# A fused attention and mixer kernel: the second channel product's seven products in transposed form, wider sums, packed constants

## The chip, the cores and the metric

The kernel runs on one core of a Trainium2 chip. The metric is device time in microseconds (us) of one execution, the median of several runs; lower is better. The core's engines are TensorE (PE: matmuls, with its weight loads shown apart as PEld), VectorE (DVE), ScalarE (ACT), GpSimd (POOL) and SyncE (SP, which here only issues transfers). Matmuls write PSUM, a small memory that VectorE and ScalarE read; all else lies in SBUF, 128 partitions wide. Transfers are carried by 16 DMA engines.

## What is computed

The inputs are u and v (8 batches, 3008 positions, 256 channels), z (8, 3008, 64) and four weights. An attention without softmax is gated by u, and a mixer follows that mixes first over positions (tokens), then over channels:

```python
# _attn_ref
scale = 1.0 / S
scores = scale * np.matmul(z, z.transpose(0, 2, 1))
attn = np.maximum(scores, 0.0) ** 2
out = np.matmul(attn, v)
return (u * out).astype(np.float32)
...
# _moe_ref, x is the result above
xt = x.transpose(0, 2, 1)
h = np.maximum(xt @ w_tok1, 0.0) @ w_tok2          # (3008 -> 256 -> 3008)
u = x + h.transpose(0, 2, 1)
h2 = np.maximum(u @ w_ch1, 0.0) @ w_ch2            # (256 -> 1536 -> 256)
return (u + h2).astype(np.float32)
```

Operands are bf16, sums in PSUM are float32.

## The kernel before

**Tiling.** The 3008 positions of a batch are six blocks of 512 (the last has 448); `b` counts batches, `q` query blocks, `g` key blocks. A key tile is 128 positions, four of them make a group.

**Attention.** `score_run` (line 448) makes score tiles in PSUM (line 465), `relu` (480) takes them to an `at` tile with ScalarE, `square` (509) squares them on VectorE (line 511). Scores are symmetric, so a block of one (q, g) is also used for (g, q): `flip` (558) turns a whole `at` tile into an `fl` tile by a transposing transfer on SyncE's queue (line 562), and blocks on the diagonal are completed by smaller turns (`flip_tiles`, line 554). `av_matmul` (684) accumulates attention times v (line 692). `finish` and `gate` (804, 836) add the two halves and multiply by u into `xT`, channels in partitions. `turn_x` (879) turns that back into an `x_pair`, positions in partitions.

**Token mixing.** The product with w_tok1 is done by a scheme with seven products of half-size blocks in place of eight. The scheme needs sums of blocks: `token_sums` (949) makes them of the weights once, `x_sums` (908) of the data, four subtractions for each block into a `d_pair` (line 921). `tok1` (1008) runs the products into one PSUM pair `a_ps` (line 1031); `collect_a` (1040) adds the parts into a float32 tile `a_f` and writes the relu into a tile of its own, `a_sb`. `tok2` (1099) multiplies by w_tok2 into `h_ps` (line 1105), its `add` (line 1114) adds to `xT`. `turn_u2` turns the sum into `u_sb`, positions in partitions.

**Channel mixing.** `ch1` (1149) makes 256 hidden channels at a time, in six steps `c2` (line 1162), and ScalarE writes their relu into `h2pre` tiles (line 1201), each of which holds two steps (a channel group `d`). The product with w_ch2 is again the seven-product scheme, for every block but the very last of the kernel: `mix_weights` (974) makes the weight sums once (line 990, eight subtractions), `make_sums` (1227) the sums of the hidden values, four instructions for each group into an `hsum` tile (lines 1241, 1246, 1250, 1253). `product` (1272) runs one of the products k = 1 to 7, each 12 matmuls of 128 columns (six in the last block), into one of two PSUM banks, `xb` or `zb` (line 1298), and `collect` (1309) adds the bank to the output tile `ro` with VectorE (line 1334) after each. When all seven are in, the tile is stored (line 1339). The rest goes through plain products (`ch2`, line 1398, stores at line 1436).

A hidden tile is cut in four for the scheme: by channels into two halves `r` and by positions into two halves `m`. Before, `m` runs over alternate tiles of 128 positions:

```python
            return st["h2", q, d].rearrange("p (j r) w -> p j r w", r=2)[
                :, :, r, :2 * n * P].rearrange("p j (i m s) -> p j i m s", m=2, s=P)[:, :, :, m, :]
```

**What sets the order.** There is no dynamic scheduler on the chip. While the program is built, a planner keeps estimated clocks for each engine: `push` (364) puts an operation for ScalarE, VectorE or SyncE on a list with an estimated ready time, a busy time and a latency; `run_engines` issues those whose time has come; the loop from line 1778 picks TensorE's next work by what the estimates say is ready. The products of a block and the hidden steps of the next are one list in a fixed order, line 1510, where 0 stands for a hidden step of the next block and 1 to 7 for a product:

```python
                for k in ORDER_LAST[b % 2] if q == NQ - 1 else (0, 0, 1, 2, 0, 6, 5, 0, 7, 3, 0, 4):
```

**Buffers and queues.** SBUF tiles come from pools with a set number of places, counted in `ROOM`: 11 `fl`, 9 `xT`, 6 `at`, 6 `h2`. The `fl` places hold flipped attention tiles, `x_pair`, `d_pair`, `hsum`, `ro` and `a_f` in turn; `release` gives a place back at an estimated time. SyncE's queue carries all turns and the stores, in the planner's order. GpSimd's queue carries the loads of u, v, z and the weights; `after` (122) puts a copy of one column into a tile `mark` in front of a load, so that the load starts only when that column is there. The z tiles of a batch are loaded into `zs` (26 columns of 64 values each, the first and the last zero) and turned by `turn_z` (136) in pairs of transfers that start at tile k and k + 1 (line 141).

**Constants.** `mark` is 128 bytes per partition and comes first, then the weights, their sums, an identity matrix `ident` and `zs`.

Of the kernel before, what the change touches and what calls it, by code (L numbers as in the profile page):

```python
# [57 lines left out]
def kernel(  # L58
# [29 lines left out]
    sb = ctx.enter_context(tc.tile_pool(name="sb", bufs=2))  # L88
    psum = ctx.enter_context(tc.tile_pool(name="psum", bufs=2, space=bass.MemoryType.PSUM))
# [7 lines left out]
    mark = consts.tile([P, 32], F32)  # L97
# [83 lines left out]
    def turn_on_pe(zr, zp):  # L181

        for t in range(GK):
            nc.tensor.matmul(  # L184
                zp[:, t, :], zr[:, t].rearrange("p h d -> p (h d)"), ident[:],
                start=(t == 0), stop=True, skip_group_check=True)
# [15 lines left out]
    def fill(n, bank):  # L202

        for _ in range(n):
            nc.tensor.matmul(
                bank, zero[:, :P], zero[:], start=True, stop=True, skip_group_check=True)
# [672 lines left out]
    def turn_x(b, q, t):  # L879
# [10 lines left out]
        push("dve", t + slack, 0.21, 0.36, lambda t: x_sums(b, q, t), first=-1,  # L890
# [17 lines left out]
    def x_sums(b, q, t):  # L908


        if q % 2 == 0:
            d_pairs[b, q] = new_pair(xd_home(b, q), [3, QW // P // 2, P], "d_pair")
# [4 lines left out]
        steps = [(d[:, 1], high[:, 1], low[:, 1]), (low[:, 1], low[:, 1], low[:, 0]),  # L917
                 (d[:, 0], high[:, 1], low[:, 1]), (d[:, 2], high[:, 0], d[:, 0])]
# [55 lines left out]
    def mix_weights(t):  # L974
# [5 lines left out]
        for c in range(2):  # L980
# [3 lines left out]
                (to[:, 0], low[:, :, 1, :], low[:, :, 0, :]),  # L984
                (to[:, 2], high[:, :, 1, :], low[:, :, 1, :]),
                (to[:, 1], high[:, :, 1, :], to[:, 0]),
                (to[:, 3], high[:, :, 0, :], to[:, 1])]

        def step(t):
            nc.vector.tensor_sub(*steps.pop(0))  # L990
# [5 lines left out]

    BORROW = 3
    VERY_LAST = (B - 1, NQ - 1, CHT // 2 - 1)
    ORDER_LAST = ((1, 2, 6, 5, 7, 0, 3, 4), (1, 2, 6, 5, 0, 7, 3, 0, 4))

    def add_mixer(b):
# [6 lines left out]
        def tok1(q, end):  # L1008
# [10 lines left out]
            for i in range(n):  # L1019
# [4 lines left out]
                    ((1, 1), w[:, j, 0, 1, :], xp[:, 1, i, 0, :]),  # L1024
                    ((0, 2), w_sum_sb[:, 1, j, :], d[:, 0, i, :]),
                    ((1, 2), w_sum_sb[:, 0, j, :], d[:, 1, i, :]),
                    ((0, 3), w_sum_sb[:, 2, j, :], xp[:, 1, i, 1, :]),
                    ((1, 0), w[:, j, 1, 1, :], d[:, 2, i, :]),
# [8 lines left out]
            if q == NQ - 1:  # L1037
                home = "fl" if b else "h2"

                def collect_a(t):  # L1040
# [35 lines left out]
                    def relu_a(m, t):  # L1076
# [7 lines left out]
                        if len(made) == 2:  # L1084
                            recent[0] = to[:, :1]
                            if b:
                                release("fl", [1], max(made))
                            else:
                                live["h2"] -= 1

# [8 lines left out]
        def tok2(q, end):  # L1099
# [9 lines left out]
            def add(t):  # L1109
# [13 lines left out]
                u_done[q].t = t  # L1123
                st["turned", q] = push("sp", t, 1.25, 5.5, lambda t: turn_u2(q, t), first=1,
                                       room=lambda: has_room(("us",)) and (
                                           q <= HALF or goal[0] > (b, 1 + HALF)))
            ring.append((push("dve", end + 0.21, 1.12, 1.25, add, first=2), slot))

# [20 lines left out]
        def ch1(q, c2, borrowed, end):  # L1149
# [64 lines left out]
            if c2 == CHT // 2 - 1:  # L1214
                release("xT", xT_uses[q])

# [4 lines left out]
        def tiles_of(q, d, r, m):  # L1221

            n = pairs_of(q)
            return st["h2", q, d].rearrange("p (j r) w -> p j r w", r=2)[
                :, :, r, :2 * n * P].rearrange("p j (i m s) -> p j i m s", m=2, s=P)[:, :, :, m, :]

        def make_sums(q, d, t):
# [6 lines left out]
            def kind(k):  # L1234
                return sums["s"][:, k, :, :n, :]

            def add1(t):
                home, n_home = take_home(q)
                sums["s"] = sb.tile([P, 4, 2, 2, P], BF16, tag=home, name="hsum", bufs=n_home)
                st["sum", q, d] = sums["s"]  # L1240
                nc.vector.tensor_add(kind(0), tiles_of(q, d, 0, 1), tiles_of(q, d, 1, 1))  # L1241
                push("dve", t - 0.05, busy, busy + 0.15, add3, done=s_done[q, d, 2])
# [679 lines left out]
```

## Time and profile before

| | us |
|---|---|
| median of 3 runs | 1113.02 |
| lowest, highest | 1112.36, 1117.03 |
| span of the profiled execution, first to last instruction | 1110.5 |
| TensorE busy in it | 1105.7 |
| VectorE busy | 782.5 |
| ScalarE busy | 669.4 |
| GpSimd busy | 164.3 |

The profile is one execution; for that one it gives the span and no time outside it, so the median is set beside the span. Every view below comes from this execution. A row of a group names the line, the engine, the operation, output and inputs, the shape (partitions x elements, type) and the count; then the busy time in us and the mean of one in ns; then the idle time just before them and what ended it. A row of waits gives who waited for whom, us in total, times and the longest. A row of a timeline gives start and duration in us. The chain of waits is followed back from the last instruction, so its shares say which engine set the time.

### The profile page before, as it was taken

The numbers are of one execution on the slowest core, as the hardware profiler recorded it, in microseconds if no ns is written. First come the engines' busy times: TensorE is split into PE (matmuls) and PEld (weight loads), VectorE is DVE, ScalarE is ACT, GpSimd is POOL, SyncE is SP. The second block draws the span as 40 slices with busy tenths as digits, with TensorE's granted clock in tenths as the row PEclk, the third lists the DMA queues.
The fourth block names the chain that finished last, engine by engine and source line by source line (L and its number), as shares of the span: only waits on it lengthen the run. The fifth ranks groups of instructions, "written<-read, shape, count | busy, mean of one in ns | idle before, by whom it ended". The sixth has DMA issues, their size and how long they took to land.

```text
span 1110.5 us, 27244 instructions
## 1 busy us (share of the span) xinstructions
PE 1105.7 (100%) x11073; PEld 683.8 (62%) x11073; DVE 782.5 (70%) x1888; ACT 669.4 (60%) x843; POOL 164.3 (15%) x382
## 2 busy tenths in 40 slices
PE   9999999999999999999999999999999999999998
PEld 3444575766557665576556865557655676556676
DVE  6889865975758857588566885578756777556775
ACT  7999555645854567545665456653666536743454
POOL 5320110221003110032100311003210120000100
PEclk9999999999999999999999999999999999999999
DMA  9999947796977969779697797967979678693222
GB/s 177 155 194 164 192 98 143 141 174 134 191 133 141 180 148 174 133 147 203 135 183 119 131 214 139 172 123 152 202 154 170 111 148 182 127 164 93 67 58 96
DMA packets 465725, 165.54 MB, mean 149 GB/s; under 512 B 433024, under 2 KB 448960, under 8 KB 465600
## 3 DMA queue, kind: packets, MB, share of 16 engines
q1 hardware_dynamic: 436208, 131.11, 58.6%
q0 software_dynamic: 28880, 32.32, 21.2%
q8 instruction: 86, 1.41, 0.5%
q10 hardware_dynamic: 512, 0.38, 0.1%
q14 instruction: 39, 0.32, 0.1%
HBM read 65.40 MB, written 24.64 MB: 81 GB/s over the span
## 4 chain that ended last, share of the span: by engine, by line
PE 99%; DMA 1%; issue 0%; POOL 0%; DVE 0%; POOLq 0%
PE acc L692 42%; PE hp L1162 22%; PE xb L1298 11%; PE zb L1298 8%; PE sc L465 6%; PE h_ps L1105 4%; PE a_ps L1031 3%; PE op L1398 2%; PE first_acc L609 1%; DMA v_sb<-in_v_dram 1%; PE zp L184 0%; PE up L1700 0%; DVE res L1433 0%; POOL ident masks.py:199 0%; POOL ident masks.py:197 0%
## 5 line engine op out<-in xcount | busy, mean ns | idle before, releaser
L1201 ACT ACTIVATE h2pre<-hp 128x1024 bf16<-128x1024 f32 (+1 forms) x287 | 278.5, 1008 | 204.0 <-PE hp L1162 171.5
L692 PEld LDWEIGHTS <-v_sb 64*128 64x128 bf16 x4418 | 246.3, 94 | 210.9
L692 PE MATMUL acc<-at,v_sb 64*128 64x512 bf16 (+1 forms) x2738 | 340.9, 375 | 0.0
L503 ACT ACTIVATE at<-sc 128x1024 bf16<-128x1024 f32 (+1 forms) x290 | 286.6, 1027 | 62.5 <-PE sc L465 54.8
L1162 PE MATMUL hp<-xT,w_ch_sb 128*128 128x512 bf16 (+1 forms) x1152 | 274.7, 375 | 0.0
L511 DVE TENSOR_TENSOR at<-at 128x1024 bf16<-128x1024 bf16 (+1 forms) x290 | 198.2, 687 | 103.8 <-ACT at L503 99.9
L692 PE MATMUL acc<-fl,v_sb 64*128 64x512 bf16 (+1 forms) x1680 | 192.5, 367 | 0.0
L1162 PEld LDWEIGHTS <-w_ch_sb 128*128 128x128 bf16 x1152 | 105.6, 98 | 98.1 <-issue 3.0
L1298 PEld LDWEIGHTS <-hsum 128*128 128x128 bf16 x2088 | 124.4, 98 | 18.2 <-issue 0.3
L465 PE MATMUL sc<-zT 64*128 64x512 bf16 (+1 forms) x732 | 131.8, 359 | 0.2 <-ACT zT L1750 0.2
L1298 PEld LDWEIGHTS <-h2pre 128*128 128x128 bf16 x1566 | 95.5, 98 | 20.1
L820 ACT COPY cp<-acc 128x512 f32<-128x512 f32 (+1 forms) x94 | 54.9, 584 | 77.8 <-PE acc L692 66.8
L826 DVE TENSOR_TENSOR cp<-acc,cp 128x512 f32<-128x512 f32 (+1 forms) x94 | 63.5, 676 | 50.7 <-ACT cp L820 50.1
L1241 DVE TENSOR_TENSOR hsum<-h2pre 128x512 bf16<-128x512 bf16 (+1 forms) x141 | 56.1, 402 | 40.7 <-ACT h2pre L1201 39.4
L491 ACT ACTIVATE at<-sc 128x512 bf16<-128x512 f32 (+3 forms) x152 | 56.2, 447 | 41.5 <-PE sc L465 41.0
L1298 PE MATMUL xb<-w_mix_sb,hsum 128*128 128x128 bf16 x1044 | 73.7, 219 | 0.0
L1334 DVE TENSOR_TENSOR ro<-xb,u_sb 128x256 f32<-128x256 f32 (+1 forms) x141 | 56.5, 401 | 22.5 <-PE xb L1298 20.5
L542 DVE TENSOR_TENSOR at<-at 128x512 bf16<-128x512 bf16 (+3 forms) x152 | 41.5, 321 | 38.2 <-ACT at L491 38.2
L465 PEld LDWEIGHTS <-zT 64*128 64x128 bf16 x732 | 42.8, 94 | 41.2 <-issue 3.6
L124 POOL CAST mark<-at 128x1 f32<-128x1 bf16 x24 | 8.2, 342 | 372.5 <-DVE at L511 372.5
L846 DVE TENSOR_TENSOR xT<-cp,uT 128x512 bf16<-128x512 f32 (+1 forms) x94 | 62.5, 665 | 0.9
L1253 DVE TENSOR_TENSOR hsum<-h2pre,hsum 128x512 bf16<-128x512 bf16 (+1 forms) x141 | 56.6, 401 | 2.3
(89 smaller groups left out, 968.4 us busy)
## 6 DMA issues: line engine op xcount, KB each, us to landing
out_dram<-ro SPq DMA_DIRECT2D x40, 512.0 KB, 3.0
v_sb<-in_v_dram POOLq DMA_DIRECT2D x40, 256.0 KB, 4.6
ur<-in_u_dram POOLq DMA_DIRECT2D x40, 256.0 KB, 4.9
w_tok_sb<-in_moe_w_tok_dram POOLq DMA_DIRECT2D x10, 256.0 KB, 10.7
zs<-in_z_dram POOLq DMA_DIRECT2D x35, 64.0 KB, 3.8
at<-at SPq DMA_TRANSPOSE x114, 2.4
out_dram<-ro SPq DMA_DIRECT2D x7, 256.0 KB, 3.5
fl<-at SPq DMA_TRANSPOSE x105, 4.7
```

The lines of the kernel that those rows point to most:

```text
L465: nc.tensor.matmul(sc[:, r, c0:c1], zT[h, k:k + P], zT[h, m + c0:m + c1], start=True, stop=True)
L491: nc.scalar.activation(a3[:, i, c0:c1], sc[:, r, c0:c1], ACT.Relu, scale=inv_S)
L503: nc.scalar.activation(view, sv, ACT.Relu, scale=inv_S)
L511: nc.vector.tensor_mul(view, view, view)
L692: nc.tensor.matmul(o, vs[blk.b, g][rows, i, dh * P:(dh + 1) * P], rhs, start=(dh, h) not in blk.begun, stop=stop, skip_group_check=True)
L826: nc.vector.tensor_add(cp[:, :W], acc[:, 0, :W], cp[:, :W])
L846: nc.vector.tensor_mul(xT[:, dh, :full * P].rearrange("p (t s) -> p t s", s=P), acc[:, :full * P].rearrange("p (t s) -> p t s", s=P), uT[: ...
L1162: nc.tensor.matmul(hps[r % len(hps)][:, r, :W], w_ch1_sb[:, dc, cc * P:(cc + 1) * P], xT[:, dc, :W], start=(dc == 0), stop=(dc == DT - 1))
L1201: nc.scalar.activation(h2[:, :, :W], hp[:, :, :W], ACT.Relu)
L1253: nc.vector.tensor_sub(kind(3), tiles_of(q, d, 1, 0), kind(1))
L1298: nc.tensor.matmul(to[:, i * P:(i + 1) * P], lhs, weights[:, c2, :], start=(first_use and c2 == 0 and i == 0), stop=(c2 == CHT // 2 - 1), ...
L1334: nc.vector.tensor_add(res(m, h), source, us(m, h) if opening else res(m, h))
```

## The change

It has these parts.

- **Sums of the hidden values.** Positions are now halved into a first and a second half of the block (`quarters`), and the sums take another, transposed form of the same scheme: the first two are the differences of the second and first position half, for both channel halves in one instruction of twice the width; the third and the fourth follow from these. Three instructions instead of four, with the planner's busy time of the first set to 0.62.
- **Products.** Numbers 3 and 4 swap raw and summed operands and their weights, 6 and 7 swap their sums, and the places of the output to which 3, 4 and 6 add move with it. Order, sizes and count stay. The `hsum` tiles are released after product 4 instead of product 7.
- **Weight sums.** Eight instructions as before, two of them additions.
- **Sums for the token product.** The same step there: one double-width difference in place of two; `d_pair` holds four parts instead of three, and `x_pair` is no longer written.
- **Packing.** The identity lies behind the zeros in one tile; `a_sb` lies in the last two parts of `a_f`, whose place is released when the token stage has ended; `zs`, the weight sums of the second channel product and the room for sums of w_ch1 share one tile, in which the zero columns of `zs` overlap its neighbours.
- **Marker.** `mark` becomes a single float32 column, allocated behind all other buffers, in a pool of its own.
- **Grouped hidden products.** New functions for the first channel product in seven products come with it (`hidden_weights`, `token_quarters`, `grouped_ch1`, `add_grouped`); `grouped` returns False for every block, so they are not called.

```diff
-    mark = consts.tile([P, 32], F32)
+    mark = marks.tile([P, 1], F32)
...
-    w_mix_sb = consts.tile([P, 4, CHT // 2, P], BF16)
...
-    ident = consts.tile([P, P], BF16)
-
-    zs = consts.tile([P, KT + 2, d_qk], BF16)
+    HID, MIX = 8 * P, 4 * (CHT // 2) * P
+    shared_sb = consts.tile([P, HID + KT * d_qk + MIX], BF16)
+    w_hid_sb = shared_sb[:, :HID].rearrange("p (k j c) -> p k j c", k=4, c=P)
+    w_mix_sb = shared_sb[:, HID + KT * d_qk:].rearrange("p (k c d) -> p k c d", k=4, d=P)
+    zs = shared_sb[:, HID - d_qk:HID + (KT + 1) * d_qk].rearrange("p (t d) -> p t d", d=d_qk)
...
-        steps = [(d[:, 1], high[:, 1], low[:, 1]), (low[:, 1], low[:, 1], low[:, 0]),
-                 (d[:, 0], high[:, 1], low[:, 1]), (d[:, 2], high[:, 0], d[:, 0])]
+        steps = [(d[:, 0:2], v[:, 1].rearrange("p j r d -> p r j d"), low),
+                 (d[:, 2], high[:, 1], d[:, 0]), (d[:, 3], high[:, 0], d[:, 2])]
...
-                (to[:, 0], low[:, :, 1, :], low[:, :, 0, :]),
-                (to[:, 2], high[:, :, 1, :], low[:, :, 1, :]),
-                (to[:, 1], high[:, :, 1, :], to[:, 0]),
-                (to[:, 3], high[:, :, 0, :], to[:, 1])]
+                (nc.vector.tensor_add, to[:, 0], low[:, :, 1, :], high[:, :, 1, :]),
+                (nc.vector.tensor_sub, to[:, 2], low[:, :, 0, :], low[:, :, 1, :]),
+                (nc.vector.tensor_sub, to[:, 1], to[:, 0], low[:, :, 0, :]),
+                (nc.vector.tensor_sub, to[:, 3], high[:, :, 0, :], to[:, 1])]
...
-                        st["a"] = sb.tile([P, 2, D], BF16, tag="a", name="a_sb", bufs=1)
+                        st["a"] = f[:, 6:8, :].rearrange("p k d -> p (k d)").bitcast(
+                            BF16).rearrange("p (m d) -> p m d", m=2)
...
+        def grouped(q, d=0):
+
+            return False
...
+        def quarters(q, d):
+
+            w = pairs_of(q) * P
+            tile_ = st["h2", q, d]
...
+            return tile_[:, :, :2 * w].rearrange("p (j r) (m n) -> p r m j n", r=2, m=2)
...
-                nc.vector.tensor_add(kind(0), tiles_of(q, d, 0, 1), tiles_of(q, d, 1, 1))
-                push("dve", t - 0.05, busy, busy + 0.15, add3, done=s_done[q, d, 2])
-                push("dve", t, busy, busy + 0.15, add2, done=s_done[q, d, 1])
+                h = quarters(q, d)
+                nc.vector.tensor_sub(sums["s"][:, 0:2, :, :n * P], h[:, :, 1], h[:, 0])
+                s_done[q, d, 1].t = t
+                push("dve", t - 0.05, busy, busy + 0.15, add2, done=s_done[q, d, 2])
 
             def add2(t):
-                nc.vector.tensor_sub(kind(1), kind(0), tiles_of(q, d, 0, 0))
-                push("dve", t, busy, busy + 0.15, add4, done=s_done[q, d, 3])
+                nc.vector.tensor_sub(kind(2), quarters(q, d)[:, 1, 1], kind(0))
...
             def add3(t):
-                nc.vector.tensor_sub(kind(2), tiles_of(q, d, 0, 0), tiles_of(q, d, 0, 1))
-
-            def add4(t):
-                nc.vector.tensor_sub(kind(3), tiles_of(q, d, 1, 0), kind(1))
-
-            push("dve", t, busy, busy + 0.15, add1, room=(home_of(q),), frees=frees_of(q),
+                nc.vector.tensor_sub(kind(3), quarters(q, d)[:, 1, 0], kind(2))
+
+            both = 0.62 if n == 2 else 0.34
+            push("dve", t, both, both + 0.15, add1, room=(home_of(q),), frees=frees_of(q),
                  done=s_done[q, d, 0])
...
-            raw = {1: (0, 0), 2: (1, 0), 4: (1, 1)}
-            mixed = {5: 0, 6: 1, 7: 2, 3: 3}
+            raw = {1: (0, 0), 2: (1, 0), 3: (1, 1)}
+            mixed = {5: 0, 7: 1, 6: 2, 4: 3}
...
-            if k == 7:
                 for d in range(CHT // 4):
                     release(home_of(q), [1], end + 0.2)
...
-    zero = sb.tile([P, QW], BF16, tag="h2", name="zero", bufs=ROOM["h2"])
-    nc.vector.memset(zero[:], 0.0)
+    zero_ident = sb.tile([P, QW + P], BF16, tag="h2", name="zero", bufs=ROOM["h2"])
+    zero, ident = zero_ident[:, :QW], zero_ident[:, QW:]
+    nc.vector.memset(zero, 0.0)
```

More of the change, by code (lines that the diff above doesn't have):

```diff
@@ L205, in fill @@
             nc.tensor.matmul(
-                bank, zero[:, :P], zero[:], start=True, stop=True, skip_group_check=True)
+                bank, zero[:, :P], zero, start=True, stop=True, skip_group_check=True)
     def load_v(b, c):
@@ L1230, in make_sums @@
+        def make_sums(q, d, t, last=None):
             n = pairs_of(q)
@@ L1456, in add_ch1, with add_grouped @@
                                key=(b, 2 + by)))
+        def add_grouped(q, d, stage, by):
+            if stage == 0:
+                h2_done[q, 2 * d] = h2_done[q, 2 * d + 1] = Done()
+            needs = [t_done[q], hid_done] if stage == 0 else [g_done[q, d, stage - 1]]
+            tails.append(Piece((2 if stage == 3 else 4) * column_time(QW // 2), needs,
+                               lambda end: grouped_ch1(q, d, stage, end),
+                               room=("h2",) if stage == 0 else (), key=(b, 2 + by),
+                               slot=stage == 0))
         def halves(q):
@@ L1505, in add_mixer @@
                 add_next(q, q)
+            if q + 1 < NQ and grouped(q + 1):
+                added[q + 1] = 2
             rest = [(half, i) for half in halves(q) for i in range(pieces_of(q, half))]
```

182 lines of the change are left out of this document (150 added, 32 removed).

## The prediction

> **What bounds the kernel now.** I read the page first: busy shares, the row of the granted clock, the DMA queues, the chain that ended last.
>
> ```profile
> span 1110.5 us, 27244 instructions
> ...
> PE 1105.7 (100%) x11073; PEld 683.8 (62%) x11073; DVE 782.5 (70%) x1888; ACT 669.4 (60%) x843; POOL 164.3 (15%) x382
> ...
> PEclk9999999999999999999999999999999999999999
> ...
> q1 hardware_dynamic: 436208, 131.11, 58.6%
> q0 software_dynamic: 28880, 32.32, 21.2%
> ...
> PE 99%; DMA 1%; issue 0%; POOL 0%; DVE 0%; POOLq 0%
> PE acc L692 42%; PE hp L1162 22%; PE xb L1298 11%; PE zb L1298 8%; PE sc L465 6%; PE h_ps L1105 4%; PE a_ps L1031 3%; PE op L1398 2%; PE first_acc L609 1%; DMA v_sb<-in_v_dram 1%; PE zp L184 0%; PE up L1700 0%; DVE res L1433 0%; POOL ident masks.py:199 0%; POOL ident masks.py:197 0%
> ```
>
> TensorE is busy for 1105.7 of 1110.5 us at a full granted clock, and 99% of the chain is its own. A busy TensorE need not be a TensorE at its peak, so the second question is whom it waits for. The view of waits, for TensorE alone, has three rows:
>
> ```profile
> PE wp L205 <- DVE zero L1569: 1.2, 1, 1.2
> PE first_acc L609 <- DMA v_sb<-in_v_dram: 0.4, 1, 0.4
> PE sc L465 <- ACT zT L1750: 0.2, 1, 0.2
> ```
>
> That is 1.8 us, all in the start-up, which the change leaves as it is. In the steady part TensorE waits for nobody. So a change can gain by fewer or cheaper matmuls, or lose by making one of the covered engines late; relief of VectorE alone has nothing to give.
>
> **The change part by part.** *TensorE's stream.* The built programs of both kernels have 11,073 matmuls, and by kind, size and order they are equal but for 42 places near the end of the first batch (the last query block and the one after it, where score pairs and accumulations change places). Both switch 34 times between half-height and full-height tiles. The seven products keep their sizes, their order (1, 2, 6, 5, 7, 3, 4) and their count; only which operand is raw and which is summed moves. Cost: 0 us.
>
> *VectorE.* The sums of a channel group go from four instructions to three, the first twice as wide; so do the sums of the token product.
>
> ```profile
> L511 DVE TENSOR_TENSOR at<-at 128x1024 bf16<-128x1024 bf16 x278 | 190.8, 690 | 102.1 <-ACT at L503 98.4 <-DMA fl<-at 0.2
> ...
> L1253 DVE TENSOR_TENSOR hsum<-h2pre,hsum 128x512 bf16<-128x512 bf16 x120 | 50.6, 421 | 2.0
> ...
> L1246 DVE TENSOR_TENSOR hsum<-hsum,h2pre 128x512 bf16<-128x512 bf16 x120 | 50.3, 419 | 0.0
> L1250 DVE TENSOR_TENSOR hsum<-h2pre 128x512 bf16<-128x512 bf16 x120 | 50.2, 418 | 0.0
> L1241 DVE TENSOR_TENSOR hsum<-h2pre 128x512 bf16<-128x512 bf16 x120 | 50.1, 422 | 26.5 <-ACT h2pre L1201 26.2
> ...
> L921 DVE TENSOR_TENSOR d_pair<-x_pair 128x256 bf16<-128x256 bf16 x96 | 25.5, 289 | 0.1
> ...
> L921 DVE TENSOR_TENSOR d_pair<-x_pair,d_pair 128x256 bf16<-128x256 bf16 x48 | 13.2, 287 | 0.1
> ...
> L1241 DVE TENSOR_TENSOR hsum<-h2pre 128x256 bf16<-128x256 bf16 x21 | 6.1, 288 | 14.2 <-ACT h2pre L1201 13.2 <-DMA out_dram<-ro 1.0
> ```
>
> The last number before the second bar is the mean of one in ns. The wide sum is new; the nearest row is the square, 128x1024 in bf16 too, at 690 ns. So each of the 120 full groups saves 2 x 0.420 - 0.690 = 0.15 us (18.0 us); each of the 21 half-size groups 2 x 0.288 - 0.420 = 0.156 us (3.3 us); each of the 48 token blocks, where two of 0.289 become one of the 128x512 kind, 0.158 us (7.6 us). VectorE should fall by 28.9 us, from 782.5 to about 754 us, in 189 fewer instructions. The weight sums stay eight. None of that is on the path, so 0 us of the span; the two bounds are 0 and TensorE's whole idle time, 1110.5 - 1105.7 = 4.8 us, and I take 0 because no row above names VectorE after the start.
>
> *What a sum's lateness would cost.* A wider first sum ends later, and product 5 can be late for it. The timeline of one product stage shows the last group of a block:
>
> ```profile
> 649.05 0.42 DVE L1241 TENSOR_TENSOR hsum<-h2pre 128x512 bf16<-128x512 bf16 x1 [0.16 <-ACT h2pre L1201]
> ...
> 649.39 0.42 DVE L1250 TENSOR_TENSOR hsum<-h2pre 128x512 bf16<-128x512 bf16 x1
> ...
> 649.73 0.42 DVE L1246 TENSOR_TENSOR hsum<-hsum,h2pre 128x512 bf16<-128x512 bf16 x1
> ...
> 650.62 0.41 DVE L1253 TENSOR_TENSOR hsum<-h2pre,hsum 128x512 bf16<-128x512 bf16 x1
> ...
> 651.61 0.83 PE L1298 MATMUL xb<-w_mix_sb,hsum 128*128 128x128 bf16 x12
> ...
> 654.48 0.83 PE L1298 MATMUL zb<-w_ch_sb,hsum 128*128 128x128 bf16 x12
> ...
> 656.02 0.83 PE L1298 MATMUL xb<-w_mix_sb,h2pre 128*128 128x128 bf16 x12
> ```
>
> Product 6 begins at 651.61 and needs the third sum of this group, over at 649.73 + 0.42 = 650.15: 1.5 us of cover. Afterwards it needs the second instruction, over at 649.05 + 0.69 + 0.42 = 650.16: the same. Product 5 follows 0.67 us behind product 6 and needs only the first, over at 649.74. The last sum served product 3 at 654.48 and now serves product 4 at 656.02, 1.5 us later. The cover stays or grows: 0 us. If the wide sum took twice its row (1.38 us), product 6's sum would end at 650.85, still 0.8 us early.
>
> *Buffers held longer.* The group's three sum tiles are freed after product 4 instead of product 7, that is after 656.02 + 0.67 = 656.69 instead of 654.48: 2.2 us longer. The small product's result now lives in the tile of its partial sums, which therefore stays until the token stage ends. Both are buffers of the pool from which SyncE's flips of the attention tiles draw, so a flip can start later, and behind it on SyncE's queue the next transposes and stores. What covers it, in the timeline of SyncE, the readers of the flipped tiles, and the DMA issues:
>
> ```profile
> 643.49 13.70 SPq L562 DMA_TRANSPOSE fl<-at  x5
> L692 PE MATMUL acc<-fl,v_sb x80: 375/376/377, 688.5 to 719.2; 64*128 64x512 bf16 x80
> fl<-at SPq DMA_TRANSPOSE x105, 4.7
> ```
>
> The five flips are issued by 657.2, land a median 4.7 us later (661.9), and TensorE reads the first such tile at 688.5: 26 us of cover against 2.2. Cost 0 us. The order of SyncE's instructions changes in one place (a turn of u ahead of one flip), GpSimd's in none.
>
> *Packed constants and addresses.* The marker tile, 128 bytes ahead of everything, becomes 4 bytes behind everything, so the base of every buffer moves from a multiple of 256 bytes to 128 past one; the z staging area, at 1920 bytes inside the shared tile, stays on a multiple. Sharing brings no new wait: the waits per line in the two built programs agree for the z loads but for one, and for the weight sums. Whether the shift costs anything is the one open price. The trace holds a test: the z turns go in pairs, of which the first starts on a multiple of 256 bytes and the second one z tile, 128 bytes, further. Two pairs, from the view of that line:
>
> ```profile
> L141 SPq DMA_TRANSPOSE zT<-zs x1: 1209/1209/1209, 159.0 to 159.0; - x1
> DMA to landing us min/median/max: 2.6/2.6/2.6
> L141 SPq DMA_TRANSPOSE zT<-zs x1: 1220/1220/1220, 160.4 to 160.4; - x1
> DMA to landing us min/median/max: 2.8/2.8/2.8
> L141 SPq DMA_TRANSPOSE zT<-zs x1: 1212/1212/1212, 137.1 to 137.1; - x1
> DMA to landing us min/median/max: 2.5/2.5/2.5
> L141 SPq DMA_TRANSPOSE zT<-zs x1: 1283/1283/1283, 138.3 to 138.3; - x1
> DMA to landing us min/median/max: 3.4/3.4/3.4
> ```
>
> 2.6 against 2.8 us, and 2.5 against 3.4 in a pair with other traffic: between 8 and 36% more, of which the quieter pair is the better witness. At 8% the flip lands 0.4 us later, against 26 us of cover: 0 us. For TensorE the second half of the token weights starts 6016 bytes into its tile, 128 past a multiple, and the token stage reads both halves as its moving operand:
>
> ```profile
> 156.53 2.59 PE hp L1162 x12
> 500.82 2.59 PE h_ps L1105 x12
> ```
>
> Twelve matmuls take 2.59 us in the chain where all operands are aligned (hp) and where half are not (h_ps). So 0 us here too; the rows resolve 0.01 us in twelve, 0.8 ns for each, or 9 us over 11,073, to either side. That both bounds.
>
> **The sum.** 1110.5 + 0 (matmuls) + 0 (sums) + 0 (buffers) + 0 (addresses) = 1110.5 us of span, and the median of the runs lies 1113.02 - 1110.5 = 2.5 us above it: 1113.0 us. The code for grouped hidden products is dead, since its switch always answers no.
>
> **The rivals.** *The DMA engines fill* (slower). Reads that start 128 bytes off cost more in every transpose. The queue rows decide when: 58.6% of the engines' time is q1's and 21.2% q0's, so together they reach 100% of the span once q1's share grows by 20.2 / 58.6, a good third. At the worst pair's 36% it would be 0.586 x 1.36 + 0.212 = 1.009 of the span, 1120.5 us, and 1123 with what lies outside; each further tenth on q1 adds 65 us. For it: the pair at 138.3. Against: the quiet pair's 8%, and 0.4 us as the only DMA wait of TensorE. [...]
>
> *A flip comes late at every change of batch* (slower). The 2.2 us of longer hold, in full, at seven changes: 15 us, 1128 us. It decides where a flip's cover is under 2.2 us; the shown one has 26.
>
> *VectorE was a hidden brake* (not slower). All idle time goes: 1113.0 - 4.8 = 1108.2 us. Against it: the list of waits.
>
> *The shift alters the matmuls' pace.* At the 0.8 ns that the rows cannot exclude, 1104 or 1122 us; weight loads at such a start have no row at all.
>
> **How the numbers follow.** No change 0.72; hidden brake 0.05; DMA engines 0.07; late flips 0.06; pace 0.10, half to each side. Half a percent is 5.6 us, about what a measurement of this kernel can tell from no change, so the first two are "same" (0.77), the faster pace is "faster" (0.05), the rest "slower" (0.18). The range runs from 1108, the hidden brake, to 1121, short of the full price of the DMA engines (1123), of the late flips (1128) and of the slower pace (1122): it leaves out most of these three and the faster pace, about 0.2.
>
> **What would show it.** VectorE's busy time near 754 us with 189 fewer instructions shows the sums right; a wide sum well over 690 ns shows its price wrong. A list of waits for TensorE that stays at three rows and 1.8 us shows the cover right; a row against DMA fl<-at would show the late flips, a row against hsum the late sum. Transposes that land as before (4.7 us for flips), and q1 near 58.6%, show the addresses free; q1 near 79% would show the engines full. h_ps and hp at 2.59 us for twelve show the pace. I am wrong if TensorE's busy time itself moves.

## The result, and the profile after

The changed kernel takes 1125.99 us (median of 4 runs, 1124.81 to 1129.78), the kernel before beside it 1113.32 us (1112.36 to 1117.03). The ratio is 1.0116, with a 95% interval of 1.0091 to 1.0142: slower by 10 to 16 us, where no change was forecast. The page of the changed kernel, in the parts that were shown of before:

```profile
span 1122.8 us, 26957 instructions
...
PE 1107.3 (99%) x11000; PEld 685.5 (61%) x11073; DVE 776.6 (69%) x1699; ACT 668.5 (60%) x843; POOL 169.6 (15%) x382
...
q1 hardware_dynamic: 436208, 131.11, 63.5%
q0 software_dynamic: 28880, 32.32, 21.2%
...
PE 89%; DMA 6%; DVE 2%; ACT 1%; issue 1%; SPq 0%; ACTq 0%; DVEq 0%
```

TensorE's own work is as long as it was (1107.3 us here, 1105.7 before; some of its records are missing from this trace). TensorE's share of the chain falls from 99% to 89%, and that of transfers rises from 1% to 6%. The same packets and bytes of q1, which carries the turns and flips, take 63.5% of a longer span: 713 us instead of 651, 10% more. The view of waits for TensorE has new rows:

```profile
PE sc L471 <- ACT at L509: 3.7, 4, 2.2
...
PE acc L698 <- DMA fl<-at: 0.9, 1, 0.9
PE acc L698 <- DVE at L517: 0.7, 2, 0.4
PE sc L471 <- ACT at L497: 0.7, 1, 0.7
PE acc L698 <- DMA at<-at: 0.7, 2, 0.4
```

All name the attention buffers: ScalarE's relu (L509) finds no free `at` tile to write as long as the flip that reads it has not landed. ScalarE's timeline shows this just ahead of TensorE's longest wait (2.2 us). In the kernel before, eight relus follow each other there and none waits for a flip; in the changed kernel two of them wait 2.58 us for one:

```profile
101.46 8.31 ACT L503 ACTIVATE at<-sc 128x1024 bf16<-128x1024 f32 x8 [0.97 <-DVE xT L846]
```

```profile
114.37 1.94 ACT L509 ACTIVATE at<-sc 128x1024 bf16<-128x1024 f32 x2 [2.58 <-DMA fl<-at]
```

Where the time goes shows best at the first batch's token products, which run as soon as that batch's attention is done. The view of the tile `x_pair` gives, after the durations, the starts of the first and the last of them; the kernel before:

```profile
L1031 PE MATMUL a_ps<-x_pair,w_tok_sb x36: 218/220/231, 110.6 to 115.0; 128*128 128x128 bf16 x36
```

and the changed kernel:

```profile
L1059 PE MATMUL a_ps<-x_pair,w_tok_sb x24: 219/219/315, 116.8 to 122.6; 128*128 128x128 bf16 x24
```

So 7.6 of the 12.3 us of span are lost before 122.6 us, and 4.7 later. In the tables below, "first batch" is the last start in this row less 115.0, and "later" is the rest of the difference in span. Both are of one profiled execution, as are q1 and the GB/s. That execution is the slowest of its kernel in e4, f2 and e4 again, and the quickest in the changed kernel, s2 and others, so the two columns need not add up to the difference of the medians.

Before the first flips the loads were already behind. The view of the DMA queues in the stretch from 60 to 86 us, when weights are loaded (q0) while x is turned (q1), for the kernel before:

```profile
DMA packets 7075, 4.74 MB, mean 182 GB/s; under 512 B 3253, under 2 KB 6517, under 8 KB 7072
q0 software_dynamic: 4058, 3.96, 96.7%
q1 hardware_dynamic: 3014, 0.75, 23.7%
```

and for the changed kernel:

```profile
DMA packets 6180, 4.10 MB, mean 158 GB/s; under 512 B 2982, under 2 KB 5774, under 8 KB 6177
q0 software_dynamic: 3391, 3.37, 96.1%
q1 hardware_dynamic: 2786, 0.69, 34.6%
```

Fewer packets of q1 took 1.46 times the engines' time (34.6 against 23.7%), the loads got behind, and the rate fell from 182 to 158 GB/s. The shares add up to over 100% in both (120.4 and 130.7%), so packets overlap in time on the engines. Whether more could have been moved at such shares is tested below (f3).

### The profile page after: what moved, and what is told of

Same layout as the page of the kernel before. It is cut to its first block, busy times and chain, and to the rows that moved or that the text cites. A ratio compares the mean times of both kernels' runs of the same rounds, so it can differ in the third digit from the quotient of the medians.

```text
span 1122.8 us, 26957 instructions
## 1 busy us (share of the span) xinstructions
PE 1107.3 (99%) x11000; PEld 685.5 (61%) x11073; DVE 776.6 (69%) x1699; ACT 668.5 (60%) x843; POOL 169.6 (15%) x382
## 3 DMA queue, kind: packets, MB, share of 16 engines
q1 hardware_dynamic: 436208, 131.11, 63.5%
## 4 chain that ended last, share of the span: by engine, by line
PE 89%; DMA 6%; DVE 2%; ACT 1%; issue 1%; SPq 0%; ACTq 0%; DVEq 0%
PE acc L698 35%; PE hp L1193 21%; PE xb L1448 10%; PE zb L1448 8%; PE sc L471 6%; PE h_ps L1129 4%; PE a_ps L1059 3%; DMA fl<-at 3%; PE op L1545 2%; DMA x_pair<-xT 1%; ACT at L509 1%; PE first_acc L615 1%; DMA at<-at 1%; DVE at L517 0%; DMA out_dram<-ro 0%
## 5 line engine op out<-in xcount | busy, mean ns | idle before, releaser
L509 ACT ACTIVATE at<-sc 128x1024 bf16<-128x1024 f32 (+1 forms) x290 | 286.1, 1027 | 71.0 <-PE sc L471 58.9
L1193 PE MATMUL hp<-xT,w_ch_sb 128*128 128x512 bf16 (+1 forms) x1089 | 271.3, 374 | 3.3
L1448 PEld LDWEIGHTS <-hsum 128*128 128x128 bf16 x2088 | 127.9, 98 | 28.6 <-issue 1.0
L1384 DVE TENSOR_TENSOR hsum<-h2pre 128x1024 bf16<-128x1024 bf16 (+1 forms) x141 | 90.9, 648 | 43.4 <-ACT h2pre L1232 35.5
L1448 PE MATMUL xb<-shared_sb,hsum 128*128 128x128 bf16 x1044 | 73.6, 219 | 0.1
```

Of the source, the lines that this page charges most:

```text
L509: nc.scalar.activation(view, sv, ACT.Relu, scale=inv_S)
L1193: nc.tensor.matmul(hps[r % len(hps)][:, r, :W], w_ch1_sb[:, dc, cc * P:(cc + 1) * P], xT[:, dc, :W], start=(dc == 0), stop=(dc == DT - 1))
L1384: nc.vector.tensor_sub(sums["s"][:, 0:2, :, :n * P], h[:, :, 1], h[:, 0])
L1448: nc.tensor.matmul(to[:, i * P:(i + 1) * P], lhs, weights[:, c2, :], start=(first_use and c2 == 0 and i == 0), stop=(c2 == CHT // 2 - 1), ...
```

## The experiments

Two theories stood at the start. *Addresses*: every buffer starts 128 bytes past a multiple of 256, the turns become slower, and the flips come late. *Structure*: the moved places of TensorE, the longer held buffers, or the wide sums. The label of each run stands at its expectation. Times are medians, with the ratio to the kernel before, run beside it, and its 95% interval.

**The change without the shift.**

```diff
-    mark = marks.tile([P, 1], F32)
+    mark = consts.tile([P, 32], F32)
-    HID, MIX = 8 * P, 4 * (CHT // 2) * P
+    HID, MIX = 7 * P, 4 * (CHT // 2) * P
```

> The changed kernel with the marker as a [P, 32] tile in front again, so that every buffer starts on a multiple of 256 bytes (the unused room for hidden weights is cut to make space; the z staging area then starts 128 bytes past one). Everything else of the change stays: wider sums, sum tiles held until product 4, results of the small product in the tile of its partial sums, 42 moved places of TensorE. By the theory of the addresses (slower transposes are what makes TensorE wait): 1113 us, q1 back near 58.6%, no waits of TensorE in the steady part. By the theory of the structure (longer held buffers and the moved places at the end of the first batch): 1126 us, with q1 near 59% and the same gaps of TensorE between 95 and 120 us. Both at work: between, 1117 to 1122 us.

**The shift without the change**, in three ways: marker behind, marker in front but 256 bytes, marker in front but 64 bytes.

```diff
-    mark = consts.tile([P, 32], F32)
+    mark = marks.tile([P, 1], F32)      # e2; e3: consts.tile([P, 64], F32), e4: consts.tile([P, 16], F32)
```

> The kernel before with one edit: the marker is a [P, 1] tile in a pool of its own behind the other buffers, so that every buffer starts 128 bytes past a multiple of 256. No instruction differs but for addresses. By the theory of the addresses: 1126 us, q1 near 63.5%, waits of ScalarE's exponentials at DMA fl<-at near the end of the first batch. By the theory of the structure: 1113 us, q1 near 58.6%.

> The kernel before with the marker kept in front but widened to [P, 64], 256 bytes: again every buffer starts 128 bytes past a multiple of 256, without the marker's own move. By the theory of the addresses the same as with the marker behind: 1126 us. By a theory that the marker's place counts (its writes from GpSimd beside other data): 1113 us here and 1126 us with the marker behind. By the theory of the structure: 1113 us in both.

> The kernel before with the marker [P, 16] in front, 64 bytes: every buffer starts 192 bytes past a multiple of 256, so on an odd multiple of 64. [...]

(What the expectation of e2 calls exponentials are ScalarE's relus.)

| run | us | ratio | q1 | GB/s, 60 to 86 us | first batch | later |
|---|---|---|---|---|---|---|
| the change | 1125.99 | 1.0116 (1.0091 to 1.0142) | 63.5% | 158 | 7.6 | 4.7 |
| e1, change without shift | 1118.09 | 1.0055 (1.0028 to 1.0082) | 58.9% | 179 | 5.2 | 0.5 |
| e2, shift alone, behind | 1125.56 | 1.0116 (1.0101 to 1.0131) | 63.8% | 150 | 5.0 | 6.9 |
| e3, shift alone, front | 1124.60 | 1.0118 (1.0085 to 1.0151) | 63.7% | 178 | 0.7 | 8.8 |
| e4, marker of 64 bytes | 1126.70 | 1.0131 (1.0113 to 1.0148) | 64.3% | 168 | 5.6 | 11.5 |

The shift alone, with not an instruction changed, costs what the whole change costs. It is the addresses and not the marker's place (e3), and starts 192 bytes past a multiple of 256 cost like 128 past (e4). Not all of it can be read from TensorE's list of waits: in e2 its rows behind the start-up add up to 8.0 us, and the span grew by 11.9. The structure is not free either: e1, without the shift, still lost 5.2 us in the first batch. A part of that lies in the start-up of this execution, where TensorE waited 1.6 us for turns of z:

```profile
PE sc L471 <- DMA zT<-zr: 1.6, 2, 1.0
```

**Which buffers.** Padding tiles ahead of and behind a pool shift it alone.

```diff
+    class Padded:
+        todo = ["at", "uT"]             # s2: ["fl", "ur"]; s3: as s1, and mark [P, 64]
+
+        def tile(self, *args, tag, **rest):
+            if tag in self.todo:
+                self.todo.remove(tag)
+                pool.tile([P, 32], F32, tag="pad_" + tag, name="pad", bufs=1)
+            return pool.tile(*args, tag=tag, **rest)
+
+    pool, sb = sb, Padded()
...
+    pad = consts.tile([P, 32], F32)     # s4 instead: behind zs, and mark [P, 64]
```

> The kernel before with only the six attention buffers (at) moved 128 bytes, so that the flips fl<-at have a shifted source, the transposes at<-at a shifted source and destination, and nothing else moves. If the attention transposes carry the loss (they are 219 of the transposes that SyncE issues): 1122 to 1126 us and q1 near 63%. If the other transposes and loads carry it: 1113 us and q1 under 60%.

> The kernel before with only the eleven fl buffers moved 128 bytes: destinations of the flips, part of the x pairs, the first value tiles and part of the u tiles. If a shifted destination costs as much as a shifted source: 1117 to 1122 us, q1 near 61%. If the source alone counts: 1113 us, q1 under 59.5%.

> The kernel before with every buffer moved 128 bytes but for the six attention buffers. If the attention buffers carry the loss: 1113 to 1116 us, and q1 near 60%, all the rest being shifted. If source and destination count alike, or the loads and the small transposes: 1120 us or more, q1 over 62%.

> The kernel before with only the constants moved 128 bytes: the weights' tiles (destination of the weight loads, weights and moving operands of the matmuls) and the z staging area. If the slower weight loads of the first batch (10.7 us to 14 us at a landing) carry the loss: 1119 us or more, with the gaps of TensorE near 95 to 120 us. If the transposes do: 1113 us, q1 near 59%. A slower pace of matmuls with shifted operands would show here as well, as a longer TensorE without waits.

| run | us | ratio | q1 | GB/s, 60 to 86 us | first batch | later |
|---|---|---|---|---|---|---|
| s1, only `at` | 1117.92 | 1.0048 (1.0033 to 1.0063) | 61.4% | 172 | -0.2 | 4.8 |
| s2, only `fl` | 1116.82 | 1.0035 (1.0022 to 1.0048) | 58.4% | 165 | -0.2 | 0.0 |
| s3, all but `at` | 1120.41 | 1.0075 (1.0058 to 1.0091) | 62.1% | 169 | 4.6 | 0.7 |
| s4, only constants | 1112.54 | 0.9996 (0.9986 to 1.0006) | 58.9% | 167 | 0.3 | 0.0 |

The profile of s2 is of its quickest run (1112.27 us; eight of its ten took 1116.1 to 1119.2), so it doesn't show where that loss lies. The others, one profile each, split it in two: with `at` shifted, and only that, the losses lie at the later changes of batch, and with all but `at` shifted in the first batch. Neither expectation was met in full: the attention buffers carry some of the loss, not all. Constants alone cost nothing (0.9996, s4), so shifted destinations of the weight loads, shifted weights and shifted moving operands of the matmuls were free here where nothing else was shifted.

What a late flip does in the later batches can be read from ScalarE's timeline. Before, its diagonal block waits for the scores:

```profile
310.93 1.43 ACT L491 ACTIVATE at<-sc 128x512 bf16<-128x512 f32 x4 [3.86 <-PE sc L465]
```

In s1 the same four instructions wait for a flip:

```profile
311.64 1.43 ACT L502 ACTIVATE at<-sc 128x512 bf16<-128x512 f32 x4 [4.77 <-DMA fl<-at]
```

and TensorE's view of waits over the whole of s1 has these rows among others:

```profile
PE acc L703 <- ACT at L514: 1.3, 3, 0.7
...
PE acc L703 <- DMA at<-at: 0.4, 1, 0.4
```

The turns are not much slower for that. The DMA issues between 300 and 1100 us, with the median landing time last, before:

```profile
at<-at SPq DMA_TRANSPOSE x99, 2.4
fl<-at SPq DMA_TRANSPOSE x78, 4.7
```

and in s1:

```profile
at<-at SPq DMA_TRANSPOSE x99, 2.8
fl<-at SPq DMA_TRANSPOSE x79, 5.0
```

and in e2, where every buffer is shifted:

```profile
at<-at SPq DMA_TRANSPOSE x99, 2.6
fl<-at SPq DMA_TRANSPOSE x81, 5.1
```

By this reading the three to four tenths of a microsecond each in s1 are enough at these places. That it is the scarce `at` tiles and SyncE's queue that turn them into waits is read from the timelines, not tried by itself.

**What of the structure costs.** The planner is told a longer time for the token sums (0.34 and 0.48 us for 0.21 and 0.36). With that number put back the order of TensorE's and SyncE's instructions is that of the kernel before. f1 is e1 with the old number, f4 the kernel before with the new one.

```diff
-        push("dve", t + slack, 0.34, 0.48, lambda t: x_sums(b, q, t), first=-1,
+        push("dve", t + slack, 0.21, 0.36, lambda t: x_sums(b, q, t), first=-1,
```

> The whole change with aligned buffers as in e1_change_aligned, and one number of the planner put back: the cost and due time of the token sums, 0.34 and 0.48 us, are 0.21 and 0.36 us again. With it the order of TensorE's and SyncE's instructions is that of the kernel before, and the 42 moved places are gone. If these moved places are what e1 lost: 1112.5 us, no waits of TensorE in the steady part, and the saving on VectorE (776 for 782 us busy) is worth 0. If the longer held buffers or the wide sums cost: 1118 us, as e1.

> The kernel before with that one number alone: the token sums announced as 0.34 and 0.48 us, though they take what they took. TensorE's and SyncE's order is that of the changed kernel. If the moved places cost by themselves: 1116 to 1119 us, with a wait for the attention buffers near 110 us. If they cost only together with the new sums: 1112.5 us.

g1 is f1 with the tile `a_sb` and the early `release` of the kernel before; g2 the changed kernel, shifted, with the old number.

```diff
-                        st["a"] = f[:, 6:8, :].rearrange("p k d -> p (k d)").bitcast(
-                            BF16).rearrange("p (m d) -> p m d", m=2)
+                        st["a"] = sb.tile([P, 2, D], BF16, tag="a", name="a_sb", bufs=1)
```

> As f1_change_old_due (the whole change, aligned, old due time), and the small product's result is in a tile of its own again, so that the tile of its partial sums is freed as early as in the kernel before. f1 stands 1.6 us above the kernel before. If that tile's longer hold is what costs it: 1112.9 us. If the sum tiles held until product 4, or the wide sums, cost it: 1114.5 us as f1, with TensorE's wait for ro still listed.

> The changed kernel as it is, shifted, with the planner's old cost and due time of the token sums. If the two causes hit the same flips at the end of the first batch and so do not add up: 1125 to 1127 us, as the changed kernel. If they add up: 1121 to 1122 us.

| run | us | ratio | GB/s, 60 to 86 us | first batch | later |
|---|---|---|---|---|---|
| f1, change, aligned, old number | 1114.49 | 1.0015 (1.0005 to 1.0025) | 160 | -0.2 | 2.4 |
| f4, before, new number | 1116.38 | 1.0030 (1.0017 to 1.0042) | 167 | 4.6 | 0.5 |
| g1, f1 with the tile `a_sb` | 1114.45 | 1.0019 (1.0009 to 1.0028) | 171 | -0.1 | 2.2 |
| g2, change, shifted, old number | 1130.74 | 1.0167 (1.0139 to 1.0195) | 153 | 7.6 | 7.8 |

One number of the planner costs 3.3 us (0.0030 of 1112.9) with no other edit. TensorE's moved places and the turn of u that goes ahead of a flip on SyncE's queue come with it together; which of them costs was not tried. With the old number the aligned change is down to 1.6 us above before. g1 shows that the small product's tile is not the cause of these 1.6 us; the sum tiles and the wide sums are left. TensorE's one new wait in f1 is in the products, but it is 0.4 us of the 2.2 by which the span grew, so that part stays open:

```profile
PE xb L1448 <- DVE ro L1481: 0.4, 2, 0.3
```

With the shift the number does not cost: g2 lies above the changed kernel, with intervals that just overlap. The two don't add up, and why g2 isn't quicker is open.

How the new order costs more than its wait, in e1. TensorE's timeline and, for the four microseconds around it, the view by windows, with the granted clock third from the end:

```profile
109.84 1.03 PE L698 MATMUL acc<-at,v_sb 64*128 64x512 bf16 x8
113.02 0.39 PE L471 MATMUL sc<-zT 64*128 64x512 bf16 x2 [2.15 <-ACT at L509]
113.23 1.83 PE L698 MATMUL acc<-at,v_sb 64*128 64x512 bf16 x8
```

```profile
109.00:112.00 3.00, 1.87 (x18) 0.76 (x15) 0.69 (x1) 0.12 (x2) 0.00 (x0) 1.00 0.94 118
112.00:116.00 4.00, 2.98 (x20) 1.59 (x20) 2.67 (x5) 3.77 (x5) 0.00 (x0) 0.67 1.27 235
```

The wait takes 2.15 us. Behind it the same eight matmuls take 1.83 us instead of 1.03, and the clock was granted at 0.67 in the mean over 4 us.

**Is it full DMA engines?** f2 takes 768 KB off the shifted kernel's first batch, f3 puts 768 KB onto the aligned one's.

```diff
# f2, beside the edit of e2
-            nc.gpsimd.dma_start(
-                out=w_ch2_sb[:, c0:c0 + h, :],
-                in_=moe_w_ch2.rearrange("(cc c) d -> c cc d", c=P)[:, c0:c0 + h, :])
+            nc.gpsimd.memset(w_ch2_sb[:, c0:c0 + h, :], 0.0)
# f3: the same load once more, with out= the half of w_mix_sb that is as large
```

> The kernel before with every buffer moved 128 bytes, as in e2_shift_behind, and the two loads of the second channel weights left out: GpSimd sets that tile to zero in their place, so 768 KB less go through the DMA engines between 60 and 90 us, and the channel products run on zeros. If the loss of the first batch (5.0 us between 95 and 116 us) comes from DMA engines that are full in that stretch: most of it goes and the losses at the later batch changes stay, 1120 to 1122 us. If it comes from the shifted addresses as such, wherever the engines stand: 1125 us.

> The kernel before, aligned, with the two loads of the second channel weights issued twice, the second time into the tile that the weight sums overwrite later: 768 KB more through the DMA engines of the first batch and nothing else. If that stretch is bound by full DMA engines: 2 to 5 us more, lost between 95 and 120 us and nowhere later, 1115 to 1118 us. If the engines still have room there: 1112.5 us.

f2: 1122.22 us, ratio 1.0067 (1.0047 to 1.0087), first batch 2.7 us instead of 5.0, 154 GB/s. f3: 1112.82 us, ratio 1.0005 (0.9992 to 1.0019), first batch -0.2 us, at 193 GB/s. The ratio of f2 lies below that of e2 with intervals apart, so the relief gained something. How much of it lies in the first batch is not shown: the profile is of f2's slowest run (1126.95 us), which lost 11.8 us later, and that the products run on zeros is a difference besides. The extra load of f3 cost nothing: aligned, the engines simply moved more. So the shares of the queues' time in the kernel before, 120.4% together from 60 to 86 us, were not the limit of the bytes: f3 has 125.7%, and 193 GB/s against 182.

**Do the turns of x slow the loads?** They are the only turns that SyncE issues between 42 and 85 us. g3 is e4 with their pools aligned again, h1 the complement; g3 and e4 were repeated beside h1.

```diff
+        todo = {"h2": 16, "v": 48, "xT": 16}    # pads of 64, 192 and 64 bytes
...
+                pool.tile([P, self.todo.pop(tag)], F32, tag="pad_" + tag, name="pad", bufs=1)
...
-    mark = consts.tile([P, 32], F32)            # h1 keeps this line
+    mark = consts.tile([P, 16], F32)
```

> The kernel before with every buffer on an odd multiple of 64 bytes, as in e4_shift_64 (1126.7 us), but for the two pools that the turns of x use in the first batch: their source xT and the pool of their destination start on multiples of 256 bytes again (the last small buffers too). These turns are the transposes that run while the weights are loaded, 53 to 79 us. If their shifted packets are what makes the loads end late and with them the first flip: the loss between 95 and 116 us goes (5 us), the first flip at 86 us takes SyncE under 3 us instead of 7, and the losses at the later batch changes stay: 1119 to 1121 us. If shifted loads or the shifted flips themselves make the loss of the first batch: 1125 us or more.

> The complement of g3_shift_but_x: the kernel before, aligned, but for the pools of the turns of x (their source xT, the pool of their destination, and the last small buffers), which start 64 bytes past a multiple of 256. If these turns' shifted packets among the weight loads make the first batch's loss: 1116 to 1119 us, the first flip at 86 us takes SyncE 5 us or more, and nothing is lost at the later batch changes. If only shifted loads and flips count: 1113 us and a first flip of 1.6 us.

> g3_shift_but_x once more, in more rounds, because one execution of e3_shift_front, where the turns of x are shifted as well, showed a first flip of 1.8 us and no loss in the first batch. If the turns of x carry that loss: 1120 to 1122 us and a first flip under 3 us again. If the loss comes and goes by itself: a time as in e4 beside it.

> e4_shift_64 once more beside g3_again, on the same chip: every buffer on an odd multiple of 64 bytes. By the turns of x: 4 to 6 us above g3_again, 1125 to 1128 us. If the loss of the first batch comes and goes by itself: within 2 us of g3_again.

| run | us | ratio | GB/s, 60 to 86 us | first flip, us of SyncE | first batch | later |
|---|---|---|---|---|---|---|
| g3, shift but x | 1121.00 | 1.0089 (1.0063 to 1.0115) | 177 | 1.94 | -0.1 | 7.9 |
| g3 again | 1123.78 | 1.0103 (1.0090 to 1.0116) | 149 | 6.87 | 3.7 | 6.6 |
| e4 again, shift | 1127.35 | 1.0141 (1.0107 to 1.0174) | 130 | 10.73 | 15.3 | 9.0 |
| h1, x alone | 1113.04 | 1.0010 (1.0000 to 1.0021) | 165 | 1.63 | 0.4 | 0.0 |

The first g3 came out as the theory had it, and its repeat did not: the loss of the first batch was back with the turns of x aligned. h1 settles it: with these turns shifted alone, nothing is lost. So the turns of x are not the cause by themselves, and one profile of g3 had been luck. What holds in every profile is the order of events: the first flip is stuck where the weight loads are still under way when it is issued. SyncE's queue at the first flip, before and in e2:

```profile
85.96 1.63 SPq L562 DMA_TRANSPOSE fl<-at  x1
```

```profile
85.96 7.47 SPq L563 DMA_TRANSPOSE fl<-at  x1
```

The DMA queues from 86 to 90 us, before (no packet of q0, which carries the loads) and in e2:

```profile
q1 hardware_dynamic: 1633, 0.42, 94.8%
```

```profile
q0 software_dynamic: 842, 0.51, 122.3%
q1 hardware_dynamic: 595, 0.14, 30.0%
```

Each later flip of the first batch stands behind this one: the next three are issued from 97.27 us in e2, from 91.33 before. Eight profiles have a first flip of over 5 us: the change, e2, e4, s3, f2, g2, g3 again and e4 again. In each of them q0 moved 86 to 978 packets in these four microseconds, and the first batch lost 2.7 to 15.3 us. In the other twelve, the kernel before among them, q0 moved at most 15, the first flip took at most 2.7 us, and the first batch lost at most 0.7 us but for e1 and f4, which have the planner's new number. The mean rate from 60 to 86 us doesn't sort the runs, because it is low as well where the loads were over before 86 us: f1 has 160 GB/s and lost nothing. It also follows that f3 did not make the loads late: 15 of its packets were left. This is an order of events that twenty profiles share; that late loads hold up the flip was not made to happen by itself.

Which buffers together slow the loads is open. None of four did it alone (`at`, `fl`, the constants, x) in the one execution profiled of each, which for `fl` is its quickest, and it came and went among executions of one kernel.

## Why the prediction was wrong, point by point

- *Packed constants and addresses*, priced at 0 us. This is the step that failed: slower transfers set against a cover of 26 us. The slowing away from the loads was about as worked out: q1's packets cost 10% more over the whole span, where the quiet pair of z turns had said 8%, and the flips of e2 between 300 and 1100 us landed in 5.1 us instead of 4.7, the forecast 0.4 us later. The size among the weight loads was not: there q1's packets took 1.46 times the engines' time in the changed kernel (34.6 against 23.7% from 60 to 86 us, for fewer packets), more than the 36% of the pair that was set aside. Measured price: 12.9 us (0.0116 of 1112.46, e2).
- The two pairs of z turns were also a weak test. Two other pairs of the same trace, from 26.2 and from 251.9 us, went the other way (landed after 4.5 us aligned and 3.8 shifted, 4.6 and 4.3).
- The cover of that step, "26 us". It was read from one block in the middle of a batch, where the flip's readers come late. It is not the cover of the first flip, which stood behind the loads of the first batch, nor that of the flips at a change of batch: there ScalarE waited for an `at` tile until the flip had landed (4.77 us in s1, up to 311.64 us), and 0.3 us per flip went with a loss of 5.3 us (s1, 0.0048 of 1112.57).
- *The DMA engines fill* was the rival nearest to the truth, and its condition was wrong. It asked for a full third more of q1 over the span. The engines did not have to fill: f3 moved more (193 GB/s from 60 to 86 us) at no cost (1.0005). What counted was one stage, and whether its loads were over when the first flip was issued. A mean over 1110 us hides that; by the view of the DMA queues the kernel before had little to spare, with 582 packets of q0 from 80 to 84 us and 4 from 84 to 86, and the flip at 85.96.
- *TensorE's stream*, "42 places" at 0 us. Wrong too: with the buffers aligned, the number that moves them and a turn of u costs 3.3 us (f4), with TensorE's wait, 2.8 us there, at the end of the first batch, where the `at` tiles are short. In the changed kernel the shift is there as well, and the two don't add up.
- *VectorE*. The instruction count fell by 189 as said, the wide sum took what its row had said (686 ns against 690), but busy time fell by 5.9 us and not 28.9. The mis-sized term is the saving per group: durations were added that overlap. Four sums of the kernel before run from 647.34 to 648.88 us:

```profile
647.34 0.42 DVE L1241 TENSOR_TENSOR hsum<-h2pre 128x512 bf16<-128x512 bf16 x1
647.67 0.42 DVE L1250 TENSOR_TENSOR hsum<-h2pre 128x512 bf16<-128x512 bf16 x1
648.01 0.42 DVE L1246 TENSOR_TENSOR hsum<-hsum,h2pre 128x512 bf16<-128x512 bf16 x1
648.46 0.42 DVE L1253 TENSOR_TENSOR hsum<-h2pre,hsum 128x512 bf16<-128x512 bf16 x1
```

  Three of the changed kernel run from 657.23 to 658.84, 1.61 us instead of 1.54:

```profile
657.23 0.69 DVE L1384 TENSOR_TENSOR hsum<-h2pre 128x1024 bf16<-128x1024 bf16 x1
657.95 0.42 DVE L1389 TENSOR_TENSOR hsum<-h2pre,hsum 128x512 bf16<-128x512 bf16 x1
658.41 0.43 DVE L1402 TENSOR_TENSOR hsum<-h2pre,hsum 128x512 bf16<-128x512 bf16 x1
```

  Sums that don't need each other start 0.33 us apart though each lasts 0.42; each of the three needs the one before. That relief of VectorE is worth nothing here was right.
- *Buffers held longer*, 0 us. Right for the small product's tile (g1 against f1); for the sum tiles not settled, within the 1.6 us of f1.
- *The shift alters the matmuls' pace*: no. s4 shifts all weights, and with them the moving operands of the second token product, and takes 0.9996 of the time.

The range ended at 1121 us because the full price of the flips and of the DMA engines was put above it with little chance.

## What to carry to other kernels

A small tile put at the front or taken away moves every buffer behind it; here that cost 12.9 us with no other edit (e2). Before such an edit is priced at nothing, look at the turns' share of the DMA engines by stage, at how long before the first turn of a stage its loads are over, and at the stage in which the engine that bounds the kernel is closest to waiting for a turn; the cover of one block in mid-batch says nothing of the last one. A planner's estimate is code as well: one changed estimate moved 42 places of TensorE and a turn, and cost 3.3 us. And where a run's profile fits the theory, repeat it before the theory is believed: g3 fitted once.

## What the runs showed of the hardware

- With not an instruction changed, starts 128 bytes past a multiple of 256 raised the time of the same 436,208 packets of q1 from 651 us (58.6% of 1110.5) to 716 us (63.8% of 1122.4, e2), and starts 192 bytes past to 725 us (64.3% of 1127.6, e4).
- The first flip, issued between 85 and 89 us, took SyncE 5.3 to 10.7 us in the eight profiles where 86 packets or more of the weight loads fell between 86 and 90 us, and 1.6 to 2.7 us in the twelve where at most 15 did.
- From 60 to 86 us the DMA engines moved 193 GB/s in f3 and 130 in e4's second profile, with the queues' shares adding up to over 100% in both: such shares do not say that no more can be moved.
- A gap of TensorE of 2.15 us (e1) was followed by a granted clock of 0.67 in the mean over 4 us, and the eight matmuls behind it took 1.83 us instead of 1.03; from 95 to 125 us the mean was 0.94. In e2, where one wait of TensorE in the same 30 us took 1.7 us, the mean there stayed at 1.00.
